# Shift rows sent by SyncE, router constants moved, and cleared products on TensorE in the opening of a fused attention and mixture-of-experts kernel

## The chip, the cores and the metric

One core of a Trainium2 chip runs the whole program. The metric is the device time of one execution in microseconds, as the median of several runs; the profile comes from one further execution of its own.

## The reference, cut

Attention over 8 batches, 8 heads, 576 positions of width 64, with a causal mask and a bias from a running sum of the positive part of `s`; its output, as 4608 rows of 512, goes through a two-level router (4 groups of 4 experts) and one expert of 512 x 1024 x 512 each.

```python
scores = (q @ k.T) / np.sqrt(64)
cum = np.cumsum(np.maximum(s, 0), axis=-1)
bias = -(cum[..., :, None] - cum[..., None, :])
scores = np.where(causal, -1e9, scores + np.minimum(bias, 0))
attn = softmax(scores); x = (attn @ v), heads side by side: (4608, 512)
g = argmax(x @ w_group); e = argmax(x @ w_expert[g])
out[token] = p_g * p_e * (relu(x @ w1[g, e]) @ w2[g, e])
```

## The kernel before, in words

The 64 heads (batch and head) are taken in 32 pairs; both heads of a pair p lie in one load `raw[p]` (q and k, 576 KB). Scores are built in two operands, `WA` (four buffers; 64 rows of q or k rounded, plus four rows that carry the running sum and the negated row maximum, each split into a rounded part and a remainder) and `WB` (five buffers; remainders of q and k). So a score tile is two products, one of 68 rows (L284) and one of 128 rows (L286).

The steps. Step n (0 to 63) computes the scores of head n (`scores`, B0 to B4), their exponentials on ScalarE (`exps`, L294) and causal clearing on GpSimd (`causal`, L303), and the product of the previous head's probabilities with its values (`av`, C0 to C6, L326). Four steps ahead (LEAD = 4) runs `rowmax` of head n + 4 (A0 to A5, L228): products of 66 rows into PSUM, and on VectorE a reduction with the mask (L236). Steps -4 to -1 hold row maxima alone. When the second head of a pair has its maxima, `shift_rows` (L250) turns them by a product with the identity, `shifts` makes the rounded part `th` and the remainder `tl` on VectorE (L256, L257), and `send` copies them into rows 66 and 67 of `WA` by two DMAs (L262), before the change from ScalarE's queue. `scores` of that pair need them. The letters in the lists `ORDERS`, `FIRST` and `ORDER0` are the order of all this within a step, written out by hand: A, B, C are products, the lower-case and other letters take the next piece of work from a queue (`b` an exponential, `a` a reduction, `T`, `t`, `D` turning, rounding and sending the shift rows, `S` and `G` splitting a raw pair, `R` a step of the router).

Splitting and loading. `split(p)` rounds q and k on ScalarE (L166) and takes the remainders on VectorE (pair 0) or GpSimd (L170). `place` (pairs 0 to 3) makes ScalarE write some parts straight into `WA` and `WB` (L182). `load_a(p)` and `load_b(p)` copy the rest with DMAs from SyncE (L191, L193 and L203, L204), `load_v` the values (L207), `load_raw` the pair itself (L159). A head's copy by L191 or L204 has 288 KB (L204 only 144 where `place` wrote the rest), by L203 144 KB, by L193 4.5 KB; a pair's values have 384 KB, its raw load 576 KB.

The opening. At first SyncE starts the load of s and of raw 0 to 2. VectorE scales s (L530), scans it (L532), rounds the running sum (L533) and takes the remainder (L534) into `cumh`; `load_a` copies two rows of it per head. ScalarE's program is `place`, `split` for pairs 0 to 2. Lists in `pre` say which loads and splits follow which step: after step -2 `load_a(2)`; after step -1 `load_b(1)`, values 0, raw 3 and raw 4, and then the write of `cumh` to DRAM; after step 0 the block `place(3, 0)`, `split(3, 0)`, `split(3, 1)`, `load_a(3)`, `place(3, 1)`, `place(3, 2)`, values 1. Up to step 0 the order on TensorE, VectorE, ScalarE, GpSimd and SyncE is the order of the program; from step 1 on SyncE's order is left to the scheduler, the other four stay in program order.

The router (`Router`) needs constants: a strict upper triangle `ub` and ones `ob` in bf16 (from `uf`, `onesf`), `part` (token numbers split at 64, from an index table `n1` that GpSimd writes) and `wr_sb`, the router's weights split in two. Its generator `operands` made all of them on VectorE, a piece at each letter R from step 1 on (L745 to L757).

After attention the expert part runs on the same core, with weights streamed as 64 loads of 1 MB.

Of the kernel before, what the change touches and what calls it, by code (L numbers as in the profile page):

```python
# [8 lines left out]
F32 = mybir.dt.float32  # L9
F32R = mybir.dt.float32r  # L10
BF16 = mybir.dt.bfloat16
I32 = mybir.dt.int32
AF = mybir.ActivationFunctionType
ALU = mybir.AluOpType
# [5 lines left out]
B, H, S, D = 8, 8, 576, 64  # L20
# [101 lines left out]
def attention(tc, qk, v, s, wr, xs, st):  # L122
# [3 lines left out]
    with ExitStack() as ctx:  # L126
# [59 lines left out]
        def load_a(p, placed=False):  # L186
            w = WA[p % NA]
            hl = hls[p].bitcast(F32)
            for h in range(2):
                if h or not placed:  # L190
                    nc.sync.dma_start(w[0:64, :, h, QO:].bitcast(F32), hl[h * 64:h * 64 + 64, 0:2])  # L191
                n = 2 * p + h
                nc.sync.dma_start(w[64:66, KA, h, QO:].bitcast(F32), (cumh if p < 4 else cumd)[n:n + 1].bitcast(F32))  # L193

        def load_b(p, placed=False):
            w = WB[p % NBB].bitcast(F32)
            hl = hls.pop(p).bitcast(F32)
            for h in range(2):

                hr = slice(h * 64, h * 64 + 64)  # L200
                b = slice(1 if placed and h else 0, 2)
                if h or not placed:
                    nc.sync.dma_start(w[0:64, QA, h], hl[hr, 1])  # L203
                nc.sync.dma_start(w[64:128, b, h], hl[hr, 0::2][:, b])  # L204

        def load_v(p):
            nc.sync.dma_start(VT[p % NVT][:, :, 0:2], v[p])  # L207
# [1 line left out]
        def rowmax(n):  # L209
            p, h = n // 2, n % 2  # L210
            i = p % NA
            m = mc[p % 2]
            todo = []
            for j, (q0, rows, w) in enumerate(QT):
                if w <= 512:
                    todo.append((j, q0, rows, w, 0, w))
                else:
                    todo.insert(0, (j, q0, rows, w, 0, 288))
                    todo.append((j, q0, rows, w, 288, w - 288))

            def item(j, q0, rows, w, c0, cw):

                if n < LEAD and (j + c0) % 2:
                    ps = ps_s.tile([P, 512], F32, name=f"pm{n}_{j}_{c0}", tag="ps")
                else:
                    keep("a", 1)
                    ps = ps_m.tile([P, 512], F32, name=f"pm{n}_{j}_{c0}", tag="pm")
                nc.tensor.matmul(ps[:rows, :cw], WA[i][0:66, QA, h, QO + q0:QO + q0 + rows],  # L228
                                 WA[i][0:66, KA, h, QO + c0:QO + c0 + cw], start=True, stop=True)
                mk = mask64[0:64] if rows == 64 else mask[:, S - w + c0:S - w + c0 + cw]  # L230

                mo = m[P - rows:, h * NB + j:h * NB + j + 1]

                def most():
                    tmp = sm.tile([P, 512], BF16, name=f"mx{n}_{j}_{c0}", tag="mx", bufs=2)
                    nc.vector.tensor_tensor_reduce(out=tmp[:rows, :cw], in0=ps[:rows, :cw], in1=mk[:rows],  # L236
                                                   scale=1.0, scalar=-3.0e38 if c0 == 0 else mo,
                                                   op0=ALU.add, op1=ALU.max, accum_out=mo)
                    if h and c0:
                        push("T", p, lambda: shift_rows(p))  # L240

                push("a", n, most)

            return [lambda a=a: item(*a) for a in todo]
# [8 lines left out]
        def shifts(p, i, pt):  # L253
            th = sm.tile([10, P], F32R, name=f"th{p}", tag="th", bufs=1)
            tl = sm.tile([10, P], F32R, name=f"tl{p}", tag="tl", bufs=1)
            nc.vector.tensor_scalar(out=th, in0=pt[:10, :P], scalar1=-1.0, scalar2=None, op0=ALU.mult)  # L256
            nc.vector.scalar_tensor_tensor(out=tl, in0=pt[:10, :P], scalar=-1.0, in1=th.bitcast(F32), op0=ALU.mult,  # L257
                                           op1=ALU.subtract)

            def send():  # L260
                for r, t in ((66, th), (67, tl)):
                    nc.scalar.dma_start(WA[i][r:r + 1, QA].bitcast(F32).rearrange("o h q -> o (h q)"), t.bitcast(F32))  # L262

            push("D", p, send)

# [250 lines left out]
        cumh = c0[:BH, 0:2 * S].rearrange("p (a s) -> p a s", a=2)  # L516
        s0, r1, c2 = (c1[:BH, i * S:(i + 1) * S].bitcast(F32) for i in range(3))
        cumd = dr.tile([BH, 2, S], F32, name="cumd")
        nc.sync.dma_start(s0, s.rearrange("b h s -> (b h) s"))
        for p in range(3):  # L520
            load_raw(p)
# [4 lines left out]
        def ones(i):  # L526
            for a in (QA, KA):
                nc.gpsimd.memset(WA[i][64:66 if a == QA else 68, a].bitcast(F32).rearrange("p h q -> p (h q)"), 1.0)  # L528

        nc.vector.tensor_scalar(out=r1, in0=s0, scalar1=0.0, scalar2=8.0, op0=ALU.max, op1=ALU.mult)  # L530

        nc.vector.tensor_tensor_scan(out=c2, data0=r1, data1=r1, initial=0.0, op0=ALU.add, op1=ALU.max)  # L532
        nc.vector.tensor_copy(cumh[:, 0], c2)  # L533
        nc.vector.tensor_tensor(out=cumh[:, 1], in0=c2, in1=cumh[:, 0].bitcast(F32), op=ALU.subtract)  # L534
        ones(0)

# [12 lines left out]
        make_identity(nc, ident)  # L549
        ones(1)  # L550
        ones(2)
        place(0, 0)
        split(0, 0)
        split(0, 1)
        load_a(0, True)
        split(1, 0)
        split(1, 1)
# [2 lines left out]
        place(1, 0)  # L560
        load_a(1, True)
        load_b(0, True)
        rt = Router(tc, ac, late, end, small, ring, wr_f, wr_sb, xs, st)
        place(1, 1)
        place(1, 2)
        place(2, 0)
# [31 lines left out]
        for step in range(-LEAD, NH + 5):  # L598
# [35 lines left out]
                f(*args)  # L634
            if step == -1:
                nc.sync.dma_start(cumd, cumh.bitcast(F32))
                rt.queue.append(rt.operands())
            if step == 62:
                manual.close()
# [55 lines left out]
class Router:  # L695


    def __init__(self, tc, ac, sm, end, ps_t, ps_s, wr_f, wr_sb, xs, st):
        self.end = end
        self.tc, self.sm, self.ps_t, self.ps_s, self.xs, self.st = tc, sm, ps_t, ps_s, xs, st  # L700
        self.wr_f, self.wr_sb = wr_f, wr_sb
        self.queue = []
        self.done, self.wait = -1, 0
        self.logged = -1
        self.lg = {}
        nc = tc.nc
        V = nc.vector

        def iota(name, pattern, base=0, cm=0, dt=F32):
            t = ac.tile([P] + [n for _, n in pattern], dt, name=name)  # L710
            nc.gpsimd.iota(t, pattern=pattern, base=base, channel_multiplier=cm, allow_small_or_imprecise_dtypes=True)
            return t


        onesf = end.tile([P, P], F32, name="onesf", tag="rows", bufs=1)
        nc.gpsimd.memset(onesf, 1.0)
        uf = sm.tile([P, P], F32, name="uf", tag="xrt", bufs=1)
        nc.gpsimd.affine_select(out=uf, in_=onesf, pattern=[[1, P]], compare_op=ALU.is_gt, fill=0.0,
                                base=0, channel_multiplier=-1)
        self.ub = ac.tile([P, P], BF16, name="ub")  # L720
        self.ob = ac.tile([P, P], BF16, name="ob")

        self.desc = iota("desc", [[-1, 4]], base=4)
        self.real = iota("real", [[0, NB * 5], [-1, 4]], base=4)
        self.lT = ac.tile([P, 512], F32, name="lT")
        self.cols = iota("cols", [[1, P]])
        self.thr = iota("thr", [[1, NL + 1]], dt=BF16)
        self.logit = [ac.tile([P, NB, 20], F32, name=f"logit{i}") for i in range(2)]
        for t in self.logit:
            nc.gpsimd.memset(t, 0.0)  # L730
        nc.gpsimd.memset(st.hot[:, 0, NB], 0.0)
        nc.gpsimd.iota(st.ie, pattern=[[1, E]], base=0, channel_multiplier=0, allow_small_or_imprecise_dtypes=True)

        n1 = iota("n1", [[S, B], [P, NB]], base=1, cm=1, dt=I32)
        self.part = ac.tile([P, 2, B, NB], F32, name="part")
        ni = ac.tile([P, B, NB], I32, name="ni")
        self.n1, self.ni, self.uf, self.onesf = n1, ni, uf, onesf

    def operands(self):
        V, ni, n1 = self.tc.nc.vector, self.ni, self.n1  # L740
        G = self.tc.nc.gpsimd
        G.memset(self.lT, 0.0)
        G.memset(self.real[64:P, 20:25], 0.0)
        yield 5
        V.tensor_copy(self.wr_sb[:, :, 0:20], self.wr_f)  # L745
        V.tensor_tensor(out=self.wr_sb[:, :, 20:40], in0=self.wr_f, in1=self.wr_sb[:, :, 0:20].bitcast(F32),
                        op=ALU.subtract)
        yield
        V.tensor_copy(self.ub, self.uf)
        yield  # L750
        V.tensor_copy(self.ob, self.onesf)
        yield
        V.tensor_scalar(out=ni, in0=n1, scalar1=6, scalar2=None, op0=ALU.arith_shift_right)
        V.tensor_copy(self.part[:, 0], ni)
        yield
        V.tensor_scalar(out=ni, in0=n1, scalar1=63, scalar2=None, op0=ALU.bitwise_and)
        V.tensor_copy(self.part[:, 1], ni)  # L757

    def step(self, now=False):

# [1037 lines left out]
```

## Time and profile before

| what | value |
|---|---|
| three runs, us | 867.61, 871.92, 872.62 |
| median, us | 871.92 |
| the profiled execution, us | 869.25 |
| its span on the core, us | 867.4 |
| mean granted TensorE clock | 0.996 |
| instructions | 17805 |

The profile's times are microseconds from the start of the span. PE is TensorE's products, PEld its weight loads, DVE VectorE, ACT ScalarE, POOL GpSimd, SP SyncE; a q behind an engine's name (ACTq, SPq) is its sequencer, as for the issue of a DMA. L262 is line 262 of the kernel. An arrow reads "output from input". The ends of products are modelled, so a product's duration is rough; its start is measured.

### The profile page before, as it was taken

How to read it: one execution, taken by the hardware profiler on the slowest of the kernel's cores; microseconds unless marked ns; L12 is line 12 of the kernel's file. 1: busy time of each engine (PE TensorE's matmuls, PEld its weight loads, DVE VectorE, ACT ScalarE, POOL GpSimd, SP SyncE). 2: the span in 40 equal slices, each digit the busy share in tenths (PEclk: the TensorE clock that was granted, in tenths of full speed). 3: DMA queues.
4: the chain of work that ended last, by engine and by line, in shares of the span. 5: the costliest groups of instructions: out<-in, count | busy, mean ns of one | idle time of the engine just before them, and what ended most of it. 6: DMA issues, size and time to landing. Idle time of an engine off the chain costs nothing. (4 is left out here: it accounts for less than half of the span.)

```text
span 867.4 us, 17805 instructions
## 1 busy us (share of the span) xinstructions
PE 839.2 (97%) x5601; PEld 771.9 (89%) x5601; DVE 718.4 (83%) x1982; ACT 615.0 (71%) x1393; POOL 602.5 (69%) x745
## 2 busy tenths in 40 slices
PE   4989999999999999999999999999999999999997
PEld 2778888888888888887789999999999999999996
DVE  7657788797878889787859799989999999999972
ACT  5668778786878778777747666776677777778760
POOL 9767677676876769545867756776677777777760
PEclk9999999999999999999999999999999999999999
DMA  7899898897979888633646645655566565666620
GB/s 197 266 233 250 234 235 232 213 248 194 248 209 245 236 221 225 177 87 122 194 149 225 245 151 208 205 164 193 201 201 216 188 216 195 223 228 214 215 96 26
DMA packets 82405, 174.06 MB, mean 201 GB/s; under 512 B 9692, under 2 KB 45660, under 8 KB 74112
## 3 DMA queue, kind: packets, MB, share of 16 engines
q1 hardware_dynamic: 72192, 153.20, 60.2%
q0 software_dynamic: 7488, 18.89, 5.7%
q10 hardware_dynamic: 2624, 0.76, 0.4%
q8 instruction: 46, 0.75, 0.3%
q14 instruction: 55, 0.45, 0.2%
HBM read 108.97 MB, written 19.69 MB: 148 GB/s over the span
## 5 line engine op out<-in xcount | busy, mean ns | idle before, releaser
L1067 POOL TENSOR_TENSOR wl<-raw,wh 128x512 fp32r<-128x512 f32 x163 | 209.8, 1299 | 82.5 <-ACT wh L1064 54.6
L236 DVE CUSTOM_DVE_ANT_0 mx<-pm,mask 128x192 bf16<-128x192 f32 (+4 forms) x320 | 127.3, 418 | 33.1 <-PE pm L228 30.4
L1064 ACT CAST wh<-raw 128x512 fp32r<-128x512 f32 x256 | 154.3, 616 | 0.0
L1189 PE MATMUL ph<-xh,wh 128*128 128x256 f32 (+13 forms) x512 | 140.2, 300 | 0.1
L1189 PE MATMUL ph<-xl,wh 128*128 128x256 f32 (+13 forms) x512 | 137.7, 300 | 0.1
L228 PE MATMUL pm<-WA 66*128 66x288 f32 (+4 forms) x384 | 123.8, 355 | 14.0 <-DMA WA<-ch 9.7
L284 PE MATMUL ps<-WA 68*128 68x320 f32 (+4 forms) x384 | 135.4, 356 | 1.7 <-DMA WA<-tl 1.6
L326 PE MATMUL po<-pt,VT 128*128 128x256 f32 (+3 forms) x512 | 119.0, 351 | 3.6 <-POOL pt L303 1.8
L1196 ACT ACTIVATE hh<-ph 128x256 fp32r<-128x256 f32 (+13 forms) x128 | 53.5, 418 | 85.5 <-PE ph L1189 83.3
L1269 PE MATMUL py<-hh,wh 128*128 128x256 f32 (+13 forms) x448 | 113.4, 302 | 0.1
L1269 PE MATMUL py<-hl,wh 128*128 128x256 f32 (+13 forms) x448 | 112.5, 301 | 0.0
L286 PE MATMUL ps<-WB 128*128 128x320 f32 (+4 forms) x384 | 110.2, 300 | 0.0
L1322 DVE STREAM_TRANSPOSE yr<-yT 32x384 f32<-32x384 f32 (+1 forms) x208 | 104.6, 503 | 4.5 <-ACT yT L1266 0.3
L326 PE MATMUL po<-pu,VT 128*128 128x320 f32 (+1 forms) x384 | 105.2, 382 | 0.0
L1159 DVE STREAM_TRANSPOSE xt<-xg 32x256 f32<-32x256 f32 (+1 forms) x208 | 102.3, 492 | 2.7
L326 PEld LDWEIGHTS po<-pt,VT 128*128 128x128 f32 x512 | 87.8, 191 | 16.6 <-POOL pt L303 2.5
L1189 PEld LDWEIGHTS ph<-xh,wh 128*128 128x128 f32 x512 | 95.3, 189 | 0.6 <-DVE hl L1197 0.3
L1189 PEld LDWEIGHTS ph<-xl,wh 128*128 128x128 f32 x512 | 94.7, 189 | 0.5 <-DVE xl L1142 0.3
L1189 PE MATMUL ph<-xh,wl 128*128 128x256 f32 (+13 forms) x512 | 91.9, 299 | 0.0
L170 POOL TENSOR_TENSOR WB<-r,hl 64x576 fp32r<-64x576 f32 x62 | 88.0, 1420 | 5.5 <-ACT hl L166 1.7
L228 PEld LDWEIGHTS pm<-WA 66*128 66x128 f32 (+1 forms) x384 | 68.9, 192 | 24.0 <-POOL WA L528 9.6
L422 POOL TENSOR_TENSOR xTl<-xT,xTh 128x512 fp32r<-128x512 f32 x29 | 37.0, 1275 | 75.9 <-ACT xTh L417 55.7
(255 smaller groups left out, 2001.0 us busy)
## 6 DMA issues: line engine op xcount, KB each, us to landing
raw<-in_w_dram SPq DMA_DIRECT2D x64, 1024.0 KB
r<-in_qk_dram SPq DMA_DIRECT2D x32, 576.0 KB
WA<-hl SPq DMA_DIRECT2D x60, 288.0 KB
WB<-hl SPq DMA_DIRECT2D x60, 288.0 KB
VT<-in_v_dram SPq DMA_DIRECT2D x32, 384.0 KB
WB<-hl SPq DMA_DIRECT2D x64, 144.0 KB
xs<-xr SPq DMA_DIRECT2D x15, 512.0 KB
WA<-cumd SPq DMA_DIRECT2D x56, 4.5 KB
```

What stands on the lines that cost most here:

```text
L170: (nc.vector if p < 1 else nc.gpsimd).tensor_tensor(out=hl[:, 2] if part else WB[p % NBB][0:64, KA, h], in0=r[hr, part], in1=hl[hr, part]. ...
L228: nc.tensor.matmul(ps[:rows, :cw], WA[i][0:66, QA, h, QO + q0:QO + q0 + rows], WA[i][0:66, KA, h, QO + c0:QO + c0 + cw], start=True, stop= ...
L236: nc.vector.tensor_tensor_reduce(out=tmp[:rows, :cw], in0=ps[:rows, :cw], in1=mk[:rows], scale=1.0, scalar=-3.0e38 if c0 == 0 else mo, op0 ...
L284: nc.tensor.matmul(ps[:rows, o:o + w], WA[i][0:68, KA, h, QO + k0:QO + k0 + rows], WA[i][0:68, QA, h, QO + q0:QO + q0 + w], start=True, st ...
L286: nc.tensor.matmul(ps[:rows, o:o + w], WB[p % NBB][:, KA, h, k0:k0 + rows], WB[p % NBB][:, QA, h, q0:q0 + w], start=False, stop=True)
L326: nc.tensor.matmul(po[0][:, qa - base:qb - base], VT[p % NVT].rearrange("p t a d -> p (t a d)")[:, (3 * t + 1 + h) * 64:][:, 0:P], x[:, c: ...
L1064: self.casts.append(nc.scalar.copy(h[:, j], raw[:, j]))
L1067: self.low = lows[self.u, i, j] = nc.gpsimd.tensor_tensor(out=l[:, j], in0=raw[:, j], in1=h[:, j].bitcast(F32), op=ALU.subtract)
L1159: V.transpose(dst[:, 0:n, :, j], src[:, 0:n, :, i])
L1189: self.product = nc.tensor.matmul(pss[f][:, :cap], w[f // 4][:, c, (f % 4) * P:(f % 4 + 1) * P], x[:, c, :cap], start=(c == 0 and w is sel ...
L1269: self.product = nc.tensor.matmul(pss[c][:, :cap], w[2 + f // 4][:, f % 4, c * P:(c + 1) * P], x[:, f, :cap], start=(f == 0 and w is self. ...
L1322: V.transpose(dst[:, 0:n, :, i], src[:, 0:n, :, j])
```

## The change

The shift rows' two copies are issued by SyncE. ScalarE rounds the running sum. `place(0, 0)` comes behind the two roundings of pair 0. The index table and the four conversions behind `part` go to the beginning; `ub` and `ob` become ScalarE copies after step -1; the router's first piece waits 11 letters R, not 5. `load_b(5)` waits for the last exponential of head 4 and stands behind `load_a(5)`. A cleared bf16 tile is multiplied by itself into a PSUM tile that nobody reads: 16 products at the start, 1 that waits for the rounded sum, 3 more, and one behind each product of `rowmax` for the first four heads.

```diff
 def load_a(p, placed=False):
-                nc.sync.dma_start(w[64:66, KA, h, QO:].bitcast(F32), (cumh if p < 4 else cumd)[n:n + 1].bitcast(F32))
+                st.at["wa", p] = nc.sync.dma_start(w[64:66, KA, h, QO:].bitcast(F32), (cumh if p < 4 else cumd)[n:n + 1].bitcast(F32))
 def load_b(p, placed=False):
-                if h or not placed:
-                    nc.sync.dma_start(w[0:64, QA, h], hl[hr, 1])
-                nc.sync.dma_start(w[64:128, b, h], hl[hr, 0::2][:, b])
+                copies = [nc.sync.dma_start(w[0:64, QA, h], hl[hr, 1])] if h or not placed else []
+                copies.append(nc.sync.dma_start(w[64:128, b, h], hl[hr, 0::2][:, b]))
+                for i in copies if p == 5 else ():
+                    hold(tc, i, st.at["exp", 4])
+                    behind(tc, i, st.at["wa", p])
 def rowmax(n):
                 nc.tensor.matmul(ps[:rows, :cw], WA[i][0:66, QA, h, QO + q0:QO + q0 + rows],
                                  WA[i][0:66, KA, h, QO + c0:QO + c0 + cw], start=True, stop=True)
+                if n < LEAD:
+                    stir(1)
 def shifts(p, i, pt):
             def send():
                 for r, t in ((66, th), (67, tl)):
-                    nc.scalar.dma_start(WA[i][r:r + 1, QA].bitcast(F32).rearrange("o h q -> o (h q)"), t.bitcast(F32))
+                    nc.sync.dma_start(WA[i][r:r + 1, QA].bitcast(F32).rearrange("o h q -> o (h q)"), t.bitcast(F32))
 def attention(tc, qk, v, s, wr, xs, st):
         cumd = dr.tile([BH, 2, S], F32, name="cumd")
+        still = ac.tile([P, P], BF16, name="still")
+        nc.vector.memset(still, 0.0)
+        stirred = ps_o.tile([P, 512], F32, name="stirred", tag="po").rearrange("p (a c) -> p a c", c=P)
+
+        def stir(n):
+            for _ in range(n):
+                i = nc.tensor.matmul(stirred, still, still.unsqueeze(1).to_broadcast([P, 4, P]), start=True, stop=True)
+            return i
+
+        stir(16)
         nc.sync.dma_start(s0, s.rearrange("b h s -> (b h) s"))
...
+        n1, ni = (ac.tile([P, B, NB], I32, name=n) for n in ("n1", "ni"))
+        part = ac.tile([P, 2, B, NB], F32, name="part")
+        nc.gpsimd.iota(n1, pattern=[[S, B], [P, NB]], base=1, channel_multiplier=1, allow_small_or_imprecise_dtypes=True)
+        for k, x, op in ((0, 6, ALU.arith_shift_right), (1, 63, ALU.bitwise_and)):
+            nc.vector.tensor_scalar(out=ni, in0=n1, scalar1=x, scalar2=None, op0=op)
+            nc.vector.tensor_copy(part[:, k], ni)
         nc.vector.tensor_scalar(out=r1, in0=s0, scalar1=0.0, scalar2=8.0, op0=ALU.max, op1=ALU.mult)
 
         nc.vector.tensor_tensor_scan(out=c2, data0=r1, data1=r1, initial=0.0, op0=ALU.add, op1=ALU.max)
-        nc.vector.tensor_copy(cumh[:, 0], c2)
+        rounded = nc.scalar.copy(cumh[:, 0], c2)
+        hold(tc, stir(1), rounded)
+        stir(3)
         nc.vector.tensor_tensor(out=cumh[:, 1], in0=c2, in1=cumh[:, 0].bitcast(F32), op=ALU.subtract)
...
-        place(0, 0)
         split(0, 0)
         split(0, 1)
+        place(0, 0)
         load_a(0, True)
...
             if step == -1:
                 nc.sync.dma_start(cumd, cumh.bitcast(F32))
+                nc.scalar.copy(rt.ub, rt.uf)
+                nc.scalar.copy(rt.ob, rt.onesf)
                 rt.queue.append(rt.operands())
 class Router:
     def operands(self):
         G.memset(self.lT, 0.0)
         G.memset(self.real[64:P, 20:25], 0.0)
-        yield 5
+        yield 11
         V.tensor_copy(self.wr_sb[:, :, 0:20], self.wr_f)
         V.tensor_tensor(out=self.wr_sb[:, :, 20:40], in0=self.wr_f, in1=self.wr_sb[:, :, 0:20].bitcast(F32),
                         op=ALU.subtract)
-        yield
-        V.tensor_copy(self.ub, self.uf)
-        yield
-        V.tensor_copy(self.ob, self.onesf)
-        yield
-        V.tensor_scalar(out=ni, in0=n1, scalar1=6, scalar2=None, op0=ALU.arith_shift_right)
-        V.tensor_copy(self.part[:, 0], ni)
-        yield
-        V.tensor_scalar(out=ni, in0=n1, scalar1=63, scalar2=None, op0=ALU.bitwise_and)
-        V.tensor_copy(self.part[:, 1], ni)
```

## Rows read from the trace of the kernel before

**Rows 1.** The page, part 1: busy us, share, instructions of each engine.
```profile
PE 839.2 (97%) x5601; PEld 771.9 (89%) x5601; DVE 718.4 (83%) x1982; ACT 615.0 (71%) x1393; POOL 602.5 (69%) x745
```

**Rows 2.** Stretches: length, busy us (instructions) by engine, clock, DMA share, GB/s.
```profile
10.00:20.00 10.00, 8.36 (x24) 5.34 (x24) 8.96 (x44) 6.30 (x9) 9.65 (x21) 1.00 0.83 200
20.00:30.00 10.00, 8.26 (x32) 6.90 (x31) 4.82 (x22) 5.13 (x10) 7.51 (x11) 1.00 0.98 311
...
50.00:60.00 10.00, 8.20 (x44) 7.14 (x44) 5.61 (x19) 5.45 (x14) 4.44 (x6) 0.83 0.98 231
```

**Rows 3.** Timeline, TensorE: score product B0 of steps 0, 2, 4, 6, 8.
```profile
22.21 0.55 PE L284 MATMUL ps<-WA 68*128 68x256 f32 x1 [1.57 <-DMA WA<-tl]
...
34.82 0.37 PE L284 MATMUL ps<-WA 68*128 68x256 f32 x1
...
47.86 0.52 PE L284 MATMUL ps<-WA 68*128 68x256 f32 x1
...
62.38 0.52 PE L284 MATMUL ps<-WA 68*128 68x256 f32 x1
...
73.30 0.52 PE L284 MATMUL ps<-WA 68*128 68x256 f32 x1
```

**Rows 4.** Timeline, TensorE's weight loads: one size at three times.
```profile
28.48 0.33 PEld L286 LDWEIGHTS ps<-WB 128*128 128x128 f32 x1
...
32.19 0.19 PEld L286 LDWEIGHTS ps<-WB 128*128 128x128 f32 x1
...
57.09 0.33 PEld L284 LDWEIGHTS ps<-WA 68*128 68x128 f32 x1
```

**Rows 5.** Timeline of the opening: start, length, engine, line [idle before <-releaser].
```profile
4.17 0.50 DVE L530 TENSOR_SCALAR cl<-cl 64x576 f32<-64x576 f32 x1 [4.17 <-DMA cl<-in_s_dram]
...
5.65 1.15 ACT L182 CAST WA<-r 64x1152 fp32r<-64x1152 f32 x1 [3.03 <-DMA r<-in_qk_dram]
...
7.70 0.76 SPq L193 DMA_DIRECT2D WA<-ch  x1
...
9.65 0.95 PE L228 MATMUL pm<-WA 66*128 66x288 f32 x3 [9.65 <-DMA WA<-ch]
...
16.43 1.54 ACTq L262 DMA_DIRECT2D WA<-th  x1
...
18.07 0.74 ACTq L262 DMA_DIRECT2D WA<-tl  x1
...
19.33 1.15 SPq L159 DMA_DIRECT2D r<-in_qk_dram  x2
...
26.81 1.15 ACT L182 CAST WA<-r 64x1152 fp32r<-64x1152 f32 x1
...
30.38 0.48 ACT L294 ACTIVATE pt<-ps 64x64 f32<-64x64 f32 x2
...
31.28 0.26 PEld L284 LDWEIGHTS ps<-WA 68*128 68x128 f32 x1 [0.20 <-ACT pu L294]
```

**Rows 6.** Timeline, 39 to 66 us: shift rows' issues on ScalarE and what followed.
```profile
39.05 1.16 ACTq L262 DMA_DIRECT2D WA<-tl  x1
...
40.26 0.54 ACT L294 ACTIVATE pu<-ps 128x448 f32<-128x448 f32 x1 [1.65 <-DVE mc L236]
...
54.10 0.73 ACTq L262 DMA_DIRECT2D WA<-tl  x1
...
54.87 0.38 ACT L334 ACTIVATE sums<-po 64x256 f32<-64x256 f32 x1 [3.53 <-DVE mc L236]
...
55.35 1.19 PE L326 MATMUL po<-pt,VT 128*128 128x256 f32 x2 [1.80 <-issue]
...
65.77 0.72 ACTq L262 DMA_DIRECT2D WA<-tl  x1
```

**Rows 7.** Timeline, 36 to 45 us: router's first conversion, and a wait.
```profile
36.58 1.43 DVE L749 CAST ub<-uf 128x128 bf16<-128x128 f32 x1
...
44.09 0.35 PE L228 MATMUL pm<-WA 66*128 66x192 f32 x1 [0.80 <-DVE mc L236]
```

More of the change, by code (lines that the diff above doesn't have):

```diff
@@ L562, in attention @@
         load_b(0, True)
-        rt = Router(tc, ac, late, end, small, ring, wr_f, wr_sb, xs, st)
+        rt = Router(tc, ac, late, end, small, ring, wr_f, wr_sb, part, xs, st)
         place(1, 1)
@@ L695, with __init__ @@
 class Router:
-    def __init__(self, tc, ac, sm, end, ps_t, ps_s, wr_f, wr_sb, xs, st):
+    def __init__(self, tc, ac, sm, end, ps_t, ps_s, wr_f, wr_sb, part, xs, st):
         self.end = end
@@ L732, in __init__ @@
         nc.gpsimd.iota(st.ie, pattern=[[1, E]], base=0, channel_multiplier=0, allow_small_or_imprecise_dtypes=True)
[L734 to L737, printed above, removed]
+        self.part, self.uf, self.onesf = part, uf, onesf
     def operands(self):
-        V, ni, n1 = self.tc.nc.vector, self.ni, self.n1
+        V = self.tc.nc.vector
         G = self.tc.nc.gpsimd
```

## The prediction, made before the change was run

> **What bounds the kernel now.** I read the page's busy shares first, then the table of stretches, then one score product (block 0, 256 columns) of every other step, and only then the timeline of the opening. TensorE is busy 97% of the span [rows 1], so whatever it loses early is not made up later by another engine. The score rows give the pace: from step 6 to step 8 two steps take 73.30 - 62.38 = 10.92 us, and this is the pace without router work. Before that, steps 0 and 1 take 12.61, steps 2 and 3 13.04, steps 4 and 5 14.52 us [rows 3]. So the excess over the even pace stands in three places, and the change touches each: 1.69 (more, since step 0 has no probabilities-times-values work yet), 2.12 and 3.60 us. Ahead of them the first scores of all wait 1.57 us for a DMA [rows 3]. Later pairs of steps can only shift.
>
> The table's clock column says 1.00 in the opening, but the weight loads say otherwise: the same load of 128 columns takes 0.33 us at 28.48 and 0.19 us at 32.19, and again 0.33 us at 57.09 [rows 4], in a stretch where the column does fall (0.83 over 50 to 60) [rows 2]. I therefore take TensorE to run at its lower level, 1.2 GHz, from its first product at 9.65 to about 31.5. The Trainium skill (TensorE: Matmul & The Clock Gate, Part 1) says that the lower rate is the default state and that activity releases it; the load times agree, the clock column does not show it.
>
> **The change part by part.**
>
> *Cleared products ahead of the scores (16, then 4, then one behind each of the 24 row-maximum products of steps -4 to -1).* No row has a 128x512 bf16 product. The nearest is a product of 256 columns, 0.28 us at the full and 0.55 us at the lower rate [rows 3]; twice that bounds a new one from above, 0.56 and 1.1 us, and nothing bounds it below but zero. The first 16 stand where TensorE does nothing until 9.65 [rows 5], so they cost nothing unless they take over 0.6 us each. The 24 lie in a stretch in which VectorE is busy 8.96 of 10 us against TensorE's 8.36 at the lower rate [rows 2]: VectorE's reductions set the pace, and at the full rate TensorE has over half the stretch free. 24 x 0.28 (half of the upper bound) = 6.7 us fit roughly into it. I take zero; if the clock is still low when they come, they push TensorE past VectorE, by up to 3 us.
>
> What a higher clock gives: from 22.2 to 31.5 TensorE is the pace. 9.3 us x 0.19/0.33 = 5.4, so up to 3.9 us.
>
> *Shift rows (th, tl) by SyncE.* For pair 0 the two issues now take 1.54 and 0.74 us on ScalarE's queue, and the second lands when the first scores start, 22.21 - 18.07 = 4.1 us after its issue, among the loads that SyncE has started meanwhile [rows 3, 5]. On SyncE they come in order ahead of the loads of pairs 2, 1 and 3. A small copy took 9.65 - 7.70 = 1.95 us from issue to use [rows 5]. With th ready at 16.43 and 0.76 us an issue, tl starts at 17.2 and is there at 19.1, before TensorE finishes its row maxima at 22.21 - 1.57 = 20.64. So the first scores start 1.6 us sooner; late next are the row maxima themselves.
>
> The price is on SyncE's queue. It stands still until th is ready, and behind the waiting instruction are three issues of load_a(2), three of load_b(1), values 0, raw 3 and raw 4, the cumulative sums. Seven issues of 0.58 to 0.76 us [rows 5] put raw 3's issue at about 22.5 instead of 19.33. Who waits for raw 3: ScalarE, whose block of five conversions for pair 3 (26.81 to 30.38, 3.57 us) stands in its program ahead of all exponentials of step 1. TensorE waited for the first of these at 31.28 [rows 5]. I estimate raw 3's landing: ahead of it in the queue are 288 + 288 + 144 + 144 + 384 KB, its own are 576, together 1.87 MB, at the 311 GB/s of the stretch [rows 2] 6.0 us, from about 20 on: 26.0. So the block starts 0.8 us earlier than 26.81, not 4. TensorE at the full rate then idles near 28 until step 1's exponentials.
>
> I put this whole opening, up to the start of step 2, at -0.8 us. Its ends: -1.6 - 3.9 = -5.5 if raw 3 lands before ScalarE asks for it; +1.5 if raw 3 lands at 28 or TensorE's clock falls in that wait, as it did in the idle of 1.80 us that ends at 55.35 [rows 6], and the next 3.4 us run at half speed (10 x (1 - 0.83)/0.5 by the clock column [rows 2]).
>
> *Router's constants and roundings.* Six conversions leave VectorE in steps 2 and 3, the longest taking 1.43 us [rows 7]. TensorE waited 0.80 us for VectorE at 44.09 [rows 7]. Two become ScalarE copies before the first exponential, where ScalarE is idle; four go to VectorE's start, where it waits 4.17 us for the input s [rows 5]: four of at most 1.43 us make 5.7 at most and next to nothing at least. I take half; only the upper end would delay the cumulative sums, by 1.5 us. The new wait there is for the index table on GpSimd, whose whole queue moves by that one small instruction. The rounding of the cumulative sums goes from VectorE to ScalarE, a conversion half as wide as the 1.15 us one [rows 5], about 0.6; place(0, 0) comes behind it and two more of these, 1.8 us later than its end at 6.80 [rows 5], still ahead of 9.65. Zero, with 1.5 as the bad end of both.
>
> *The same shift rows in steps 2 to 5.* On ScalarE the issue of pair 2's tl took 1.16 us at 39.05, and the next exponential came at 40.26 after 1.65 us of idle [rows 6]. With VectorE's six conversions gone too, I take 1.7 of the 2.12 us of excess in steps 2 and 3 as gained (ends 0 and 2.1). In step 4 the issue of pair 3's tl stands until 54.10, ScalarE has been idle 3.53 us when it goes on at 54.87, and TensorE goes on at 55.35 after 1.80 us, then at the lower clock [rows 4, 6]. VectorE, named as the releaser, had nothing to do with it: what was held was the issue of a DMA, in a stretch with a DMA share of 0.98 [rows 2]. Without DMAs in ScalarE's program this can't hold the exponentials. I take 3.0 of 3.60 (ends 0, if another queue's wait takes its place, and 3.6). Holding load_b(5) behind the exponentials of step 4 takes 864 KB out of just this stretch; they are wanted in step 10, so I cost the wait at nothing.
>
> *From step 6 on* the pace is TensorE's, and I take nothing; ScalarE's 1.45 us of issues a pair were covered.
>
> **Sum.** -0.8 - 1.7 - 3.0 = -5.5 us. Against the profiled execution (869.25, span 867.4) 863.75; the median of the three runs lies 2.67 above that execution, so 866.4.
>
> **The rivals.**
>
> *All three places come to the even pace.* If raw 3 is early enough and the clock holds, -5.5 - 2.1 - 3.6 = -11.2; with half a step's friction about -9.5, which is 862.4 at the median. For it: raw 3 was in use at 26.81 at the latest, and may have landed at 22 or 23. Against it: SyncE's queue, above.
>
> *The opening gives nothing.* Raw 3 lands at 28 or the products do not raise the clock in time (that the change doesn't do what it says): +1.5 - 1.7 - 3.0 = -3.2, 868.7. For it: TensorE was 8.36 of 10 us busy from 10 to 20 [rows 2] and its clock did not rise.
>
> *The stall of step 4 returns elsewhere.* SyncE is held by the same congestion and a load comes late: -0.8 - 1.7 = -2.5, 869.4.
>
> *Slower: shift rows stuck behind loads.* From pair 4 on they are issued 73.30 - 65.77 = 7.5 us ahead of their scores [rows 3, 6]. On ScalarE's queue they were alone; on SyncE's they follow whatever was issued. If issue to landing exceeds 7.5 us, each excess is paid by TensorE in each of 28 pairs: 0.6 us late makes +16.8 - 5.5, 883. For it: 4.1 us were needed in the opening even on a queue of its own. Against it: 3.4 us more are 1 MB at 311 GB/s.
> The Trainium skill (DMA: Bandwidth & Descriptors, Queues, rings and completion order) says that a DMA engine takes turns between queues and consumes one ring in order, which speaks against moving a small urgent copy to the queue of the big ones. By that rule a raw load and two WB copies ahead, 1.15 MB, would add 3.7 us to 1.95: 5.7, still inside 7.5. No run here shows it yet.
>
> **How the numbers follow.** Forecast (-3.5 to -7.5) 0.42; all at pace 0.20; opening gives nothing 0.21; stall returns 0.10; slower 0.07. The runs of before lie 5 us apart, so 1% (8.7 us) is about what a measurement of this kernel can tell from no change. Over 1% faster needs 863.2: most of the second case and a fifth of the first, 0.25. Over 1% slower, above 880.6: most of the last case, 0.05. Within 1%: 0.70. The range from 860 to 873 takes in -10.5 and the two weak cases with 2.5 us of scatter, and leaves the stuck rows out.
>
> **What would show it.** Right: in the profile after, weight loads of 0.19 us at the first scores, which start near 20.6 after no wait for tl; ScalarE's block for pair 3 starting near 26; no idle of TensorE over 1 us between steps 4 and 6; 10.9 us between the scores of steps 4 and 6 and later pairs as before. Wrong: TensorE waiting for the tl rows at the first score product of later pairs, a lower clock in step 1 or 2, or a block for pair 3 that starts after 27 or before 24.5.

## The result and the profile after

The changed kernel is slower: 878.9 us median of five executions (875.43 to 881.43) against 869.17 us for the kernel before beside them, a ratio of 1.0115, 95% interval 1.0087 to 1.0143. (A sixth execution, of 4716 us, is far from all others and counts in nothing here; with it the median is 880.0.) Two later sets of the same kernel gave 1.0089 [1.0057, 1.0120] and 1.0075 [1.0049, 1.0101]. The forecast was 866.4 in a range of 860 to 873: it had the wrong sign. The profiled execution is the quickest of the five: 875.43 us, span 873.7.

The page of the changed kernel, part 1, and its stretches (engines in the order of the first line, then the granted clock, the busy share of the DMA engines, and GB/s), to be held against [rows 1, 2]:

```profile
PE 848.8 (97%) x5645; PEld 774.9 (89%) x5645; DVE 719.8 (82%) x1980; ACT 617.2 (71%) x1396; POOL 600.7 (69%) x745
...
10.00:20.00 10.00, 9.24 (x48) 5.16 (x48) 9.39 (x47) 8.17 (x13) 9.65 (x19) 1.00 0.51 123
20.00:30.00 10.00, 7.98 (x39) 6.26 (x39) 5.13 (x26) 4.77 (x11) 7.15 (x14) 0.81 0.93 286
50.00:60.00 10.00, 9.29 (x59) 7.96 (x58) 7.57 (x28) 7.60 (x20) 6.17 (x9) 1.00 1.01 267
70.00:80.00 10.00, 6.96 (x26) 5.84 (x26) 2.78 (x13) 4.48 (x13) 5.71 (x9) 0.70 1.07 256
```

The kernel before, from 70 to 80:

```profile
70.00:80.00 10.00, 10.00 (x63) 8.83 (x62) 7.14 (x28) 8.26 (x23) 8.12 (x12) 1.00 0.99 277
```

The stretch that the old stall stood in, 50 to 60, has gained: TensorE 9.29 us busy instead of 8.20, clock 1.00 instead of 0.83. But 70 to 80 now has TensorE at 6.96 (10.00 before) and the clock at 0.70 (1.00 before), and from 10 to 20 the DMA engines moved 123 GB/s instead of 200.

Rows chosen from the timeline of the changed kernel, from 1 to 75 us; L266 is the shift rows' copy, L288 the first score product (L262 and L284 before), L529 a cleared product:

```profile
1.06 5.90 PE L529 MATMUL stirred<-still 128*128 128x512 bf16 x16 [1.06 <-DVE still L524]
...
13.82 0.70 SPq L203 DMA_DIRECT2D WB<-hl  x1
16.23 0.84 SPq L266 DMA_DIRECT2D WA<-th  x1
17.17 0.77 SPq L266 DMA_DIRECT2D WA<-tl  x1
18.04 0.65 SPq L193 DMA_DIRECT2D WA<-ch  x1
18.78 0.68 SPq L191 DMA_DIRECT2D WA<-hl  x1
...
20.18 0.20 PEld L288 LDWEIGHTS ps<-WA 68*128 68x128 f32 x1
20.22 0.47 PE L288 MATMUL ps<-WA 68*128 68x256 f32 x1
22.34 0.62 SPq L209 DMA_DIRECT2D VT<-in_v_dram  x1
23.01 1.16 SPq L159 DMA_DIRECT2D r<-in_qk_dram  x2
...
26.59 1.19 PE L330 MATMUL po<-pt,VT 128*128 128x256 f32 x2 [1.56 <-DMA VT<-in_v_dram]
28.20 1.15 ACT L182 CAST WA<-r 64x1152 fp32r<-64x1152 f32 x1 [2.70 <-DMA r<-in_qk_dram]
28.98 0.34 PEld L288 LDWEIGHTS ps<-WA 68*128 68x128 f32 x1 [0.20 <-issue]
35.59 0.56 PE L288 MATMUL ps<-WA 68*128 68x256 f32 x1
37.98 0.19 PEld L288 LDWEIGHTS ps<-WA 68*128 68x128 f32 x1 [0.20 <-ACT pt L298]
47.34 0.53 PE L288 MATMUL ps<-WA 68*128 68x256 f32 x1
59.45 0.52 PE L288 MATMUL ps<-WA 68*128 68x256 f32 x1
...
66.04 0.89 SPq L266 DMA_DIRECT2D WA<-th  x1
67.03 0.76 SPq L266 DMA_DIRECT2D WA<-tl  x1
74.36 0.55 PE L288 MATMUL ps<-WA 68*128 68x256 f32 x1 [3.04 <-DMA WA<-tl]
74.33 0.29 PEld L288 LDWEIGHTS ps<-WA 68*128 68x128 f32 x1 [3.52 <-issue]
```

Read it beside [rows 3 to 5]. Step 0 begins 1.99 us earlier, with weight loads of 0.20 us instead of 0.33: the cleared products do raise the clock. Then TensorE waits for values 0, ScalarE 2.70 us for raw 3, the loads are back at 0.34 us, and step 2 starts at 35.59 instead of 34.82. Steps 2 and 3 take 11.75 us (13.04 before), steps 4 and 5 12.11 (14.52). Then TensorE waits 3.04 us for pair 4's `tl`, issued 7.33 us before: steps 6 and 7 take 14.91 (10.92), steps 8 and 9 13.76 (10.91). At step 10 the changed kernel is 0.77 - 1.29 - 2.41 + 3.99 + 2.85 = 3.91 us behind, and at step 56 still 3.81.

The other 2.5 us of this execution are lost where attention hands over to the expert part (TensorE 7.58 us busy from 470 to 480, 10.00 before), though order and work are the same there. Over the eighteen profiles of this study the loss has two parts. One is a wait of TensorE for VectorE's `xT` near 424; first the kernel before, then the changed one (us in total, times, longest):

```profile
PE px L1139 <- DVE xT L402: 0.3, 1, 0.3
...
PE px L1150 <- DVE xT L406: 0.9, 1, 0.9
```

It is 0.7 to 0.9 us long in all nine profiles with cleared products and 0.3 in all nine without. With it the program's last product comes about 0.9 us later after step 62's first score (462.6 us, against 461.7 without products, where the second part is there too). So this part belongs to the products; by which way products of the first 20 us lengthen a wait 400 us later, no run shows. The other part, waits of 1.3 and 1.1 us near 472 and 478, costs 1.5 us. It stands in nine profiles, with products and without, and not in that of the repetition (e5), so I don't count it as the change's.

What the stretch of 12 to 26 us shows was not among my rows. The changed kernel:

```profile
12.00:26.00 14.00, 11.80 (x66) 7.37 (x64) 12.11 (x60) 9.16 (x18) 13.52 (x23) 1.00 0.65 163
```

and the kernel before:

```profile
12.00:26.00 14.00, 11.09 (x35) 7.99 (x35) 10.49 (x52) 5.48 (x10) 12.96 (x22) 1.00 0.91 256
```

The DMA share falls from 0.91 to 0.65: (0.91 - 0.65) x 14 = 3.6 us of the DMA engines' time that goes unused, because SyncE's queue stands before pair 0's `th` and every load is behind it: nothing is issued from 14.52 to 16.23, and `load_a(2)`, whose first copy the kernel before issued at 14.28, comes at 18.04. From 16 to 20 the share is 0.07 (0.86 before). From 26 to 70 it is then 0.97, against 0.90.

### The profile page after: what moved, and what is told of

It is laid out like the page before. It is cut to its first block, busy times and chain, and to the rows that moved or that the text cites. A ratio compares the mean times of both kernels' runs of the same rounds, so it can differ in the third digit from the quotient of the medians.

```text
span 873.7 us, 17943 instructions
## 1 busy us (share of the span) xinstructions
PE 848.8 (97%) x5645; PEld 774.9 (89%) x5645; DVE 719.8 (82%) x1980; ACT 617.2 (71%) x1396; POOL 600.7 (69%) x745
## 5 line engine op out<-in xcount | busy, mean ns | idle before, releaser
L288 PE MATMUL ps<-WA 68*128 68x320 f32 (+4 forms) x384 | 135.9, 358 | 3.0 <-DMA WA<-tl 3.0
L298 ACT ACTIVATE pt<-ps 128x256 f32<-128x256 f32 (+2 forms) x192 | 75.8, 397 | 10.3 <-PE ps L290 7.7
```

What stands on the lines that cost most here:

```text
L288: nc.tensor.matmul(ps[:rows, o:o + w], WA[i][0:68, KA, h, QO + k0:QO + k0 + rows], WA[i][0:68, QA, h, QO + q0:QO + q0 + w], start=True, st ...
```

## The experiments

Theory A: this gap costs the time. Theory B: the rows of later pairs cost, stuck behind loads as pair 4's `tl` was. Theory C: the cleared products cost. (In the expectations of the first runs R stands for A and B together, P for C, M for all the rest of the change. From e5 on they add D, that the bytes of the first steps bound the opening whatever TensorE does, and T, that TensorE and its waits do.) From step 1 on SyncE's order is left to the scheduler, so each edit also moves a few of its instructions; no experiment is quite free of that.

**e1, e2, e3: the change less one part.** e1 has all shift rows back on ScalarE, e2 lacks the cleared products, e3 has both edits.

```diff
 # e1, e3
-                    nc.sync.dma_start(WA[i][r:r + 1, QA].bitcast(F32)...
+                    nc.scalar.dma_start(WA[i][r:r + 1, QA].bitcast(F32)...
 # e2, e3
-                if n < LEAD:
-                    stir(1)
-        stir(16)
...
-        hold(tc, stir(1), rounded)
-        stir(3)
```

> The changed kernel with the shift rows' two copies issued by ScalarE again, all else as changed. Theory R (the rows on SyncE's queue cost the time: the queue stands until pair 0's th, so values 0 and raw 3 come late, and pair 4's tl lands 7 us after its issue): 866 to 870 us, values 0 and raw 3 wait for nobody, no idle of TensorE over 1.5 us between 60 and 80 us; the first scores wait for tl again, near 22. Theory P (the cleared products cost it, by a clock that falls once they stop): 877 to 881 still, lower clock from 26 to 37 us as in the changed kernel. Theory M (the moved router work, the rounding or the held load_b(5)): 877 to 881 too, but with the full clock in the opening.

> The changed kernel without the cleared products (none of the 16, 4 and 24; their tile is gone too). Theory R: 878 to 884, the waits for values 0, raw 3 and pair 4's tl stay where they are. Theory P: 866 to 870. Theory M: 877 to 881. By R the products' own worth is what this run loses against the changed kernel: at most 2 us, since the clock that they raise is lost again in the wait for values 0.

> The changed kernel with the rows on ScalarE and without the cleared products: only the router's moved work, the rounding on ScalarE, the order of place(0, 0) and the held load_b(5) are left. Theory R and theory P: 865 to 869, 1 to 3 us under the kernel before, since VectorE is free of six conversions in steps 2 and 3. Theory M: 877 to 881.

Measured: e1 1.0050 [1.0025, 1.0076], e2 1.0065 [1.0036, 1.0095], e3 1.0012 [0.9992, 1.0033]. So each part costs, the rows 0.53% without products (e2 less e3), the products 0.38% without the rows (e1 less e3), both just clear of the two intervals taken together; the router's moved work, the roundings and the held load, all that e3 has left, can't be told from nothing. R, P and M each gave the whole loss to one part, and none of them fits: e1 and e2 (872.4, 874.9 us) came out between the times that R and P expected, and e3 took 870.04, over the 865 to 869 of both.

**e4 and e8: one part alone, put into the kernel before.** e4 sends the rows by SyncE; e8 has the cleared products alone.

```diff
 # e4
-                    nc.scalar.dma_start(WA[i][r:r + 1, QA].bitcast(F32)...
+                    nc.sync.dma_start(WA[i][r:r + 1, QA].bitcast(F32)...
 # e8
+                if n < LEAD:
+                    stir(1)
+        stir(16)
...
+        hold(tc, stir(1), rounded)
+        stir(3)
```

> The kernel before with one edit: the shift rows' copies issued by SyncE. Theory R: 876 to 884; values 0 and raw 3 come late, and some later pair's first scores wait for tl by over 1 us. Theories P and M: 865 to 869, the first scores 1.5 us earlier and no stall of ScalarE near 54 us.

> The kernel before with the cleared products alone (16, 4, 24 of them, as in the change). Theory D: the first scores come up to 1 us earlier, the full clock holds from about 10 us, and all of it is waited off again by step 8: 868 to 871. Theory P (products at fault): 871 to 874. By the prediction's working, with the rows still on ScalarE: 866 to 868.

Measured: e4 1.0033 [1.0010, 1.0056] at a DMA share of 0.69 from 12 to 26, e8 1.0025 [1.0004, 1.0047] at 0.89. Neither part gains anything by itself. (R had expected 876 to 884 us of e4, the prediction's working 866 to 868 of e8; they took 871.68 and 870.25.)

**e5: the changed kernel again.**

> The changed kernel unchanged, for a second profile: the first one's execution took 875.4 us, the median 880. 877 to 882. Theory D (the DMA engines bound the first steps: in all six profiles so far 16.8 to 17.1 MB had been moved when step 8's first score product began, whatever TensorE had gained or lost before): step 8 again begins when about 16.9 MB are through, at 74 to 77 us. Theory R alone (waits for single rows on SyncE's queue) says nothing of the bytes and expects a wait for some tl of more than 3 us.

Measured: 1.0089, 875.53 us, below the 877 to 882 expected. Its first scores start at 20.22 again and the DMA share from 12 to 26 is 0.64. But the waits fall elsewhere. The steps of the three profiles of the changed kernel (e14 is the third, below), in us:

| | before | changed | e5 | e14 |
|---|---|---|---|---|
| steps 0 and 1 | 12.61 | 15.37 | 12.67 | 13.98 |
| steps 2 and 3 | 13.04 | 11.75 | 12.30 | 11.82 |
| steps 4 and 5 | 14.52 | 12.11 | 15.40 | 16.35 |
| steps 6 and 7 | 10.92 | 14.91 | 14.54 | 11.55 |
| steps 8 and 9 | 10.91 | 13.76 | 13.96 | 11.32 |
| step 12 begins | 96.90 | 100.81 | 101.78 | 97.76 |

In e5 and e14 the stall of step 4, gone in the first profile, is there: TensorE waits 2.31 and 3.29 us for values. So where the waits fall differs from one execution to the next, and so does what is lost by step 12: 3.91, 4.88 and 0.86 us.

**e6 and e7: the transfers of the opening, in the kernel before.** e6 loads values 0 and 1 right behind raw 2 instead of later; e7 adds two transfers of 384 KB that nobody needs.

```diff
 # e6
         for p in range(3):
             load_raw(p)
+        for p in range(2):
+            load_v(p)
...
-               -1: [(load_b, 1, True), (load_v, 0), (load_raw, 3), (load_raw, 4)],
+               -1: [(load_b, 1, True), (load_raw, 3), (load_raw, 4)],
...
 # e7
             if step == -1:
+                load_v(1)
+                nc.sync.dma_start(PT[1][0][:, 0:768], qk[31].rearrange("p a s -> p (a s)")[:, 0:768])
```

> The kernel before with the loads of values 0 and 1 issued right behind raw 2, into a stretch (8 to 10 us) in which the DMA engines were 0.10 busy. Theory D: 0.79 MB are out of the way early, so step 8 begins 1.5 to 3 us sooner than 73.3 and the time falls to 865.5 to 867 (before 868.5 over 31 runs). Theory T (TensorE and the waits in its way bound the opening, DMA has slack): 868 to 870, nothing gained, or a little lost because the running sums' copies come behind the values.

> The kernel before with two useless loads more after step -1 (values 1 a second time, and 393 KB into a tile that step 1 overwrites): 0.79 MB that nobody waits for. Theory D: 0.79 MB at 233 GB/s are 3.4 us, step 8 begins at 75.5 to 77 and the time is 870.5 to 872.5. Theory T: 868 to 869.5.

Measured: e6 1.0053 [1.0032, 1.0074]. Its first product starts at 11.29 instead of 9.65, and its first scores at 25.77 after a wait of 3.48 us for `tl`: filling the DMA engines early is worth nothing when what TensorE needs first queues behind it. e7 1.0022 [1.0003, 1.0040], 0.3 to 3.5 us for 768 KB, which take 3.3 us at the 236 GB/s of 26 to 70 us before; so the time alone leaves room for a bound by bytes. But in e7's profiled execution step 8 starts at 71.68, earlier than before (73.30) and not at the 75.5 to 77 that D expected, and e6 missed D's 865.5 to 867 as well (873.16). D is not borne out as it stood, although in the profiles without added loads 16.8 to 17.1 MB had been moved when step 8 began.

**e9, e10, e11, e12: which rows, and the held load.** e9 sends pair 0's rows alone by ScalarE, e10 pair 0's alone by SyncE, e11 drops the wait of `load_b(5)`, e12 is the kernel before with the rows of pairs 2 and 3 by SyncE.

```diff
 # e9 and e10 (in the changed kernel), e12 (in the kernel before)
+                    (nc.sync if p else nc.scalar).dma_start(...)
+                    (nc.sync if not p else nc.scalar).dma_start(...)
+                    (nc.sync if p in (2, 3) else nc.scalar).dma_start(...)
 # e11
-                for i in copies if p == 5 else ():
-                    hold(tc, i, st.at["exp", 4])
-                    behind(tc, i, st.at["wa", p])
```

> The changed kernel with the shift rows of pair 0 alone on ScalarE's queue, those of pairs 1 to 31 on SyncE's. If the loss comes from the opening, where SyncE stands still until pair 0's maxima are rounded and the DMA engines run dry from 16 to 20 us (share 0.07 in the changed kernel, 0.86 before), that share comes back to about 0.5, as with all rows on ScalarE (0.51), and the time goes to 872 to 874, half or more of the 5 us that the rows cost. If the loss comes from the rows of later pairs, which wait behind loads (pair 4: 7.3 us from issue to use), it stays at 876 to 880 and TensorE waits again for a tl between steps 2 and 9.

> The mirror of the last: pair 0's shift rows on SyncE, all others on ScalarE. By the opening's account the DMA share from 16 to 20 us stays under 0.1 and the time at 875 to 879; by the account of the later rows it is as with all rows on ScalarE, 872.

> The changed kernel without the wait of load_b(5) for the last exponential of head 4. I costed that wait at nothing: then 875 to 880 as the changed kernel. If the wait keeps SyncE's queue standing, and with it what is behind, it is 2 us or more faster than the changed kernel; if 864 KB less in steps 4 and 5 is what gave the gain there, those two steps grow by over 1 us.

> The kernel before with the rows of pairs 2 and 3 alone on SyncE: the two places where an issue on ScalarE held the exponentials, without the standing queue of the opening and without the queue of the later pairs. If those two stalls were a cost of their own, 868.3 - 4.1 = 864; if a stall removed there comes back in another step, because the transfers of the first ten steps as a whole are what is late, 868 to 870 with an idle of 2 us or more elsewhere between steps 2 and 9.

Measured: e9 1.0054 [1.0031, 1.0076], e10 1.0078 [1.0052, 1.0104], e11 1.0087 [1.0059, 1.0114], e12 0.9991 [0.9968, 1.0013]. Pair 0 alone on ScalarE does what all pairs on ScalarE did (e1, 1.0050); pair 0 alone on SyncE costs about as much as the whole change. Both times, 873.76 and 875.91 us, are those that A expected, not B. The hold costs and gains nothing that can be told. (e9's profile has the sign of B too, a wait of 2.07 us for pair 3's `tl`; its time is A's.) And e12 takes away the issues on ScalarE behind the two stalls that I had priced at 4.7 us together, and keeps the share at 0.88. In its profile steps 4 and 5 take 10.91 us and step 12 begins 2.0 us sooner than before (94.89), yet its time is 869.12 against 870.12: at most 2.8 us gained by the interval, and none resolved. The 2.0 us are not lost again in the opening, where TensorE has no wait over 1 us from step 0 to step 12 and not the 2 us of idle that I had expected: 1.4 us are left at step 62, and this profile then has the 1.5 us of waits near 472 that come and go. So a gain of one or two microseconds from these two stalls is not excluded; one of 4.7 is.

**e13 and e14: the gap filled.** In e13 all rows stay on SyncE, but values 0 and raw 3 are issued ahead of pair 0's rows; e14 is the changed kernel beside it.

```diff
         load_b(0, True)
+        load_v(0)
+        load_raw(3)
-               -1: [(load_b, 1, True), (load_v, 0), (load_raw, 3), (load_raw, 4)],
+               -1: [(load_b, 1, True), (load_raw, 4)],
```

> The changed kernel with the loads of values 0 and raw 3 issued by SyncE ahead of pair 0's shift rows instead of behind them; all shift rows stay on SyncE. If the idle DMA engines of 12 to 26 us are the cause (share 0.65 in the changed kernel against 0.91 before, over 14 us 3.6 us of transfers), the share comes back to 0.8 or more and the time to 870 to 873, although th and tl now queue behind 960 KB and the first scores start a microsecond or two later. If it is the shift rows' own lateness on SyncE's queue that costs, the time stays at 876 to 880 or rises.

> The changed kernel once more, as the bar for the run beside it: 875 to 880, DMA share of 0.65 from 12 to 26 us.

Measured: e13 1.0043 [1.0025, 1.0062], e14 1.0075 [1.0049, 1.0101]. The stretch of e13:

```profile
12.00:26.00 14.00, 12.20 (x69) 7.92 (x67) 12.12 (x60) 10.02 (x18) 13.52 (x23) 1.00 0.86 221
```

The share is back at 0.86, and e13 stands where e1 and e9 do, 0.32% below the changed kernel beside it (at the edge of the two intervals taken together), though the time expected, 870 to 873, was missed: 875.33. What is left should be the products'.

**e15 and e16: the same two cures, without the products.** e15 is e13, e16 is e9, each without the cleared products.

```diff
 # both, as in e2
-                if n < LEAD:
-                    stir(1)
-        stir(16)
...
-        hold(tc, stir(1), rounded)
-        stir(3)
```

> The changed kernel without the cleared products and with values 0 and raw 3 issued ahead of pair 0's shift rows; all shift rows on SyncE. If what the rows cost (1.0065 without products, against 1.0012 with the rows on ScalarE) is the gap in the transfers alone, the ratio to before falls to 1.000 to 1.003; if the rows of later pairs cost by themselves, it stays at 1.005 to 1.007.

> The changed kernel without the cleared products and with pair 0's shift rows alone on ScalarE. By the gap's account 1.000 to 1.003 with a DMA share near 0.8 from 12 to 26 us; by the account of the later rows 1.005 to 1.007.

Measured: e15 1.0022 [0.9999, 1.0045], e16 1.0005 [0.9986, 1.0024]: 31 of 32 pairs have their rows on SyncE in e16, and it costs nothing that can be told. Three pairs of kernels differ by the queue of these 31 alone: e3 and e16 (1.0012, 1.0005), e1 and e9 (1.0050, 1.0054), e10 and the changed kernel (1.0078; 1.0075 to 1.0115). Pair 0's rows alone make the step from e16 to e2 (1.0005, 1.0065). That their price is the gap rests on e13 and e15 (0.43% below e2, just clear of the two intervals), and the profiles leave something open there: with the share back, TensorE still waits for pair 4's `tl`, 2.75 us in e13 and in e15

```profile
75.62 0.36 PE L286 MATMUL ps<-WA 68*128 68x256 f32 x1 [3.69 <-DMA WA<-tl]
```

and both begin step 12 as late as the changed kernel (101.83, 100.66). Both profiled executions were slower than their medians (876.76, 874.59). Over all profiles TensorE waits over 1 us for pair 3's or pair 4's `tl` in eight of the ten whose rows of pairs 1 to 31 go by SyncE, and in none of the seven where they go by ScalarE. So B is there as a wait, but not as time that can be told. All runs, by the DMA share from 12 to 26 us:

| without products | share | ratio | with products | share | ratio |
|---|---|---|---|---|---|
| before | 0.91 | 1 | e8 | 0.89 | 1.0025 |
| e12 | 0.88 | 0.9991 | e13 | 0.86 | 1.0043 |
| e15 | 0.86 | 1.0022 | e9 | 0.81 | 1.0054 |
| e3 | 0.81 | 1.0012 | e1 | 0.79 | 1.0050 |
| e16 | 0.81 | 1.0005 | e10 | 0.65 | 1.0078 |
| e4 | 0.69 | 1.0033 | changed, three sets | 0.64 to 0.65 | 1.0075 to 1.0115 |
| e2 | 0.63 | 1.0065 | e11 | 0.55 | 1.0087 |

Down each column the time follows the share, as far as the intervals resolve it, and at like shares the right column lies 0.1 to 0.5% above the left. (Each share is that of one profiled execution. e6 and e7 are left out: they change what is loaded.)

**Why full clock in the opening may cost.** e9 and e16 differ by the products alone. Weight loads of e9, in time order:

```profile
22.82 0.19 PEld L288 LDWEIGHTS ps<-WA 68*128 68x128 f32 x1 [1.46 <-DMA WA<-tl]
...
58.34 0.29 PEld L288 LDWEIGHTS ps<-WA 68*128 68x128 f32 x1 [2.55 <-issue]
58.51 0.33 PEld L290 LDWEIGHTS ps<-WB 128*128 128x128 f32 x1
...
66.50 0.19 PEld L230 LDWEIGHTS pm<-WA 66*128 66x128 f32 x1
```

and of e16:

```profile
30.98 0.34 PEld L286 LDWEIGHTS ps<-WA 68*128 68x128 f32 x1 [0.20 <-ACT pu L296]
31.51 0.24 PEld L288 LDWEIGHTS ps<-WB 128*128 128x128 f32 x1 [0.20 <-issue]
...
65.85 0.33 PEld L286 LDWEIGHTS ps<-WA 68*128 68x128 f32 x1
...
69.16 0.20 PEld L288 LDWEIGHTS ps<-WB 128*128 128x128 f32 x1
```

e9 runs at the full rate from its first scores and is ahead at step 4 (44.41 against 46.37). Then TensorE waits 2.07 us for `tl` and the clock falls to its lower level, 1.2 GHz, for some 6.9 us (granted clock 0.77 from 55 to 70 us: 15 x 0.23 / 0.5); e16 falls once as well, for 3.3 us. By step 12 e9 is 1.47 us behind (96.99 against 95.52). The same in the other profiles: once their loads have shown the full rate, the kernels with products fall back to 1.2 GHz for 7 to 17 us in all (the changed one 10.2 + 6.8 by its granted clock), those without, which rise between 31 and 38 us, for 0 to 3.4. So an early fast TensorE runs into the loads, waits, and runs at half speed behind the waits.

That this is the price of the products I have not shown. No run holds the clock up through such a wait. Counted from the first scores, e16 is at the lower level for longer than e9 (from 21.91 to about 31, and 3.3 us more). And 0.93 of the 2.4 us by which e9's profile is longer than e16's lie in the handover, behind step 62.

The Trainium skill (TensorE: Matmul & The Clock Gate, "HAM oscillation — how this bites in real kernels") tells of kernels in which a wait for a DMA drops the clock, so that the work behind it starts cold again. The traces agree: 3.04 us of waiting at 74.36 in the changed kernel, and loads of 0.29 to 0.33 us from there.

## Why the prediction was wrong, point by point

*First scores near 20.6 at the full rate, no wait for `tl`.* Right: 20.22, loads of 0.20 us. But all three signs of being wrong came too: the lower clock in step 1 (loads of 0.34 us at 28.98), pair 3's block after 27 (28.20), and a wait for a later pair's `tl`.

*The opening up to step 2, -0.8.* +0.77 in the profile after, -1.93 in e5 and -0.62 in e14: near it on the mean, though -1.93 and +0.77 lie apart by more than the term itself. In the profile after raw 3 was issued at 23.01 (22.5 worked out) and used at 28.20 (26.0). My 6.0 us of transfers took 311 GB/s from 20 on; the DMA engines gave 222 GB/s from 20 to 24 in the changed kernel.

*Steps 2 to 5, -1.7 and -3.0.* In the profile after, -1.29 and -2.41. But this was one way for the waits to fall: in e5 and e14 steps 4 and 5 take 15.40 and 16.35 us. My own rival, the stall that returns elsewhere, had 0.10 and was the rule: ten of the eighteen profiles have one or two waits of TensorE of 2 to 4 us between 30 and 80 us.

*From step 6 on, nothing.* **This is the step that failed.** Steps 6 to 9 gave +3.99 and +2.85 in the profile after, +3.62 and +3.05 in e5; in e14 the loss stands in steps 4 and 5 instead (+1.83, where I had -3.0). At step 10, where the sum has -5.5, the three are 3.91, 4.88 and 1.03 us late. Beneath it lies the reading of the excess over the even pace as three stalls of fixed size, each with its own cause and each to be gained for good. As I read the runs, the loads come only just in time through the first nine steps (share 0.90 and more from 26 to 70 us), a stall is where that shows, and time won early can be lost again: e9 is 3.45 us ahead of the kernel before at step 4 (44.41) and 0.09 behind at step 12. The price that I did see, SyncE's queue standing before pair 0's rows, I followed to raw 3 and to step 2 and no further; I never asked what the DMA engines do while it stands. There lay 3.6 us of their time. That the profile after is 3.91 us late at step 10 is near it by luck: with the same gap e5 is later and e14 less late.

*The cleared products, zero with a gain at the full clock.* Wrong: they cost 0.2 to 0.5%, some 2 to 4 us. The time of the first 16 was covered, as worked out (5.90 us, below my 0.6 us each). What failed is that I counted a higher clock as a gain without asking what TensorE waits for next; and about 0.9 us of it lies at the handover, which I did not look at.

*Router's constants and roundings, zero.* Right within the measurement (e3).

*The held load_b(5), nothing.* Right (e11).

*The slower rival, rows stuck behind loads, 883.* The time came out near it and on its side, but not by its mechanism. One `tl` did take 7.33 us from issue to use, near the 7.5 that I had set as the limit and above the 5.7 that I had worked out from ring order. But such waits stand in the crowded opening (pairs 2 to 4 in the profiles), later steps run as before, and with 31 pairs on SyncE e16 costs nothing that can be told. By the Trainium skill (DMA: Bandwidth & Descriptors, "Queues, rings and completion order") a DMA engine consumes the descriptors of one ring in order; the 7.33 us agree in kind.

No version beat the kernel before by more than the interval: e12, at 0.9991, is the same.

## What to carry to other kernels

Where a wait moves to another queue, look at what that queue feeds: if the DMA engines run dry behind it, time can be lost many steps later, though every stall that you can see near the change may shrink. Stalls in a stretch with a DMA share near 1 are not to be priced one by one from a single profile: in the next execution they stand elsewhere. And a faster clock is a gain only if the next thing is there: here TensorE ran into waits, and behind its waits of 2 to 4 us it was at half speed again.

## What the runs showed of the hardware

Sixteen bf16 products of cleared operands, 128x512, took 5.90 us from 1.06 on; they multiply nothing but zeros, and still the first real weight loads found the full clock (0.19 us at 9.97 in the changed kernel). The clock column reads 1.00 from 20 to 30 us both while loads take 0.33 us (before, e16) and while they take 0.19 (e9), so there the loads are the measure. A copy of 5 KB issued at 17.17 was there within 3.05 us, one issued at 67.03 on the same queue took 7.33.
